# A gated delta rule and a gated MLP on one core: earlier masks for the triangular solve, filler matmuls, another dealing of VectorE's background work, and an early fetch for the last stage

## The chip, the core and the metric

The kernel runs on one core of one Trainium2 chip. The metric is the device time of one execution in microseconds (us). A core has five engines with their own instruction streams: TensorE (PE in the profile; its weight loads are listed as PEld), VectorE (DVE), ScalarE (ACT), GpSimd (POOL) and SyncE (SP). Transfers are issued from the queues of SP, POOL and ACT and run beside the engines.

## The reference

Two models follow one another; the output of the first is the input `x` of the second. Everything is float32.

```python
# B, H, S, D = 4, 8, 768, 48
k_n = k / (norm(k, axis=-1) + 1e-06)
state = zeros((B, H, D, D))
for t in range(S):
    y[:, :, t] = einsum('bhd,bhde->bhe', q[:, :, t], state)
    v_old = einsum('bhde,bhd->bhe', state, k_n[:, :, t])
    state = state + beta_t * einsum('bhd,bhe->bhde', k_n[:, :, t], v[:, :, t] - v_old)
x = y.transpose(0, 2, 1, 3).reshape(B, S, 384)
# d_model 384, d_ff 1024
h = gelu_tanh(x @ w_in)
u, v = h[..., :512], h[..., 512:]
v_n = (v - mean(v)) / sqrt(var(v) + 1e-06) * g_ln
v_s = einsum('ts,bsd->btd', w_sg, v_n) + b_sg[None, :, None]
out = x + (u * v_s) @ w_out
```

The first part is sequential in the 768 tokens, the spatial product `w_sg` mixes all tokens of a batch.

## The kernel before

**Chunks.** The recurrence is cut into 12 chunks of 64 tokens: six for the first two batches, six for the other two. Within a chunk the 64 steps become matrix products and the inverse of a triangular 64x64 matrix. Two chunks make a segment; the six segments have their own triangular inverses.

**Prologue.** `kload` and `qload` bring the keys and queries of a chunk (896 KB, issued on GpSimd's queue). `kgram`, `gram` and `dense` form the products of keys on TensorE, ScalarE copies them out of PSUM, `gstore` stores them to DRAM (`gd`), and `zload` brings them back with one 32x32 triangle per partition and block (`zl`). `lanes(g)` is VectorE's solve on that layout: read the diagonal, mask the upper triangle (`triu`, an affine_select on GpSimd, L317), a Newton inverse square root for the key norms, a scale, some 100 to 200 small steps over rows, outer products and columns, and a last scale. It comes in five groups: segments 0, 1, 2 with 3, 4, and 5. `zstore` stores the result (`zd`), `zfetch` brings it back as `z` and `zk`, `norms` turns the key norms into `nv`, `vprep` scales the values, `turned` transposes `zk`, and `corner_a` and `corner_b` put the off-diagonal 32x32 corners of the inverse together on TensorE.

**Turns.** The main part is a list of turns, each with a chunk c of the recurrence and a chunk f of the feed-forward part, either of which can be missing:

```python
TURNS: (0,None) (1,None) (2,None) (3,0) (None,1) (None,2) (4,3) (5,4) ... (11,10) (None,11)
```

In a turn with c the chain `old0, own0, state0, old1, own1, state1` runs, each step some 64 small matmuls that need what ScalarE or VectorE made of the step before; between the steps stand the eight `feeds` of chunk f (four `gate`, four `value`), that is matmuls with `w_in` and the gelu. In a turn without f nothing stands there. Towards the end of the turn the next chunk's `vprep`, `turned`, `corner_a` and `corner_b` follow.

**Background list.** VectorE's long work (the decoding of `w_in` into two float parts, the groups of `lanes`) waits in a list `bg`. After every step `tick` takes from it for as many estimated microseconds as the turn's entry in `SHARE` allots to the step, with an estimate per instruction of `us(n)`, 0.17 us plus n / 960. `until` takes all that is needed at once, where a turn can't go on without it (`lanes_done`). All engines work through their instructions in the order of the program, which is written by hand up to the last stage.

**Last stage.** `w_out` and `w_sg` are decoded or split by `unit`, six calls in a turn, in the last turns. After the turns come, for the four batches and two halves of tokens each, `fetch_v` (six pieces, normalised by ScalarE and VectorE), `fetch_u`, `spatial` and `project`. Here a scheduler sets the order. `keep_warm` issues matmuls of zeros whose result isn't read; before, it is called twice, 9 times at the start and 12 times ahead of turn 0 (with weights named `kick`).

## Time and profile before

| what | value |
|---|---|
| median of 3 runs | 601.35 us (600.41 to 605.57) |
| the profiled execution, its own time | 601.24 us |
| its span, first to last instruction | 599.3 us |
| mean granted TensorE clock | 0.826 of full |
| busy: TensorE, VectorE, ScalarE, GpSimd | 447.4, 360.8, 173.3, 74.7 us |
| matmuls | 7691 |
| first step of the chain of chunk 0 (L80, `ps<-v,z`) | at 86.5 us |
| last matmul of the feed-forward turns, first of the last stage | at 430.5 and 439.0 us |

The busy times are sums over stages with different limits; the profile says for each instruction group what ended the idle time before it, and in a table by stretches how busy each engine was there and which clock TensorE was granted (PEclk; 1.00 is full, 0.50 half).

### The profile page before, as it was taken

Reading aid. Unit: us, or ns where it says so; the run is one execution under the profiler, and the core shown is the slowest. Engines: PE = TensorE matmul, PEld = TensorE weight load, DVE = VectorE, ACT = ScalarE, POOL = GpSimd, SP = SyncE. Lnnn points to the kernel's source line nnn. Section 1 sums busy time; section 2 is a strip of 40 time slices with the busy share of each in tenths; the row PEclk is TensorE's granted clock in tenths of the full one; section 3 lists DMA queues with packets and bytes.
Section 4 is the critical chain, followed back from the end, with each engine's and each line's share of the span. In section 5 each row is a group of like instructions: output and inputs, shape, how many; then the busy total and the mean of one; then the engine's idle time right before and its main releaser. Section 6 shows DMA issues by size and latency. Waiting matters only on the chain.

```text
span 599.3 us, 17857 instructions
## 1 busy us (share of the span) xinstructions
PE 447.4 (75%) x7691; PEld 402.3 (67%) x7691; DVE 360.8 (60%) x1040; ACT 173.3 (29%) x382; POOL 74.7 (12%) x100
## 2 busy tenths in 40 slices
PE   4432088616948565899988991979769899999997
PEld 2432067615837454778877881868669899999997
DVE  3509583552799992766885763495645963643432
ACT  2310154112424212354424420443524421311110
POOL 3210021000030000201020100000002412222220
PEclk9655575555579875899999986997979999999999
DMA  7896285568347104886496726451787474423213
GB/s 235 179 279 159 57 211 149 115 177 170 108 125 229 70 18 133 219 233 212 118 226 193 194 84 180 121 189 47 259 231 184 125 236 132 152 56 129 83 58 118
DMA packets 99454, 92.79 MB, mean 155 GB/s; under 512 B 71600, under 2 KB 80432, under 8 KB 96912
## 3 DMA queue, kind: packets, MB, share of 16 engines
q1 hardware_dynamic: 89952, 58.40, 35.2%
q0 software_dynamic: 5312, 31.72, 19.0%
q10 hardware_dynamic: 4112, 1.54, 1.1%
q8 instruction: 60, 0.98, 0.7%
q14 instruction: 18, 0.15, 0.1%
HBM read 63.30 MB, written 28.34 MB: 153 GB/s over the span
## 4 chain that ended last, share of the span: by engine, by line
PE 52%; DVE 24%; DMA 12%; issue 6%; ACT 3%; SPq 2%; ACTq 0%; POOL 0%; DVEq 0%; POOLq 0%
PE ps L80 17%; PE ps L632 13%; PE ps L634 11%; PE ps L633 11%; DVE ztmp L357 4%; DVE zl L364 4%; DMA zd<-zl 3%; DMA kd<-kqT 3%; DMA vraw<-vD 3%; DMA gd<-gm 2%; DVE zl L351 1%; DMA z<-zd 1%; PE ps L654 1%; DVE zl L385 1%; DVE zl L341 1%
## 5 line engine op out<-in xcount | busy, mean ns | idle before, releaser
L80 PE MATMUL ps<-kd 48*64 48x128 f32 (+1 forms) x768 | 45.7, 357 | 46.8 <-DMA kd<-kqT 24.0
L80 PEld LDWEIGHTS ps<-kd 48*64 48x64 f32 x768 | 37.6, 189 | 49.6 <-ACT nv L402 21.5
L80 PEld LDWEIGHTS ps<-s,kq 48*64 48x64 f32 x1408 | 55.3, 159 | 17.6 <-issue 11.8
L80 PE MATMUL ps<-s,kq 48*64 48x48 f32 x1408 | 62.3, 245 | 4.0 <-issue 2.6
L1007 POOL TENSOR_TENSOR ga<-ga,uT 128x384 f32<-128x384 f32 x32 | 36.4, 1141 | 188.5 <-DVE ga L1004 139.9
L633 PE MATMUL ps<-xl,winh 128*128 128x256 f32 x144 | 43.4, 301 | 10.5 <-DVE xl L658 10.5
L357 DVE TENSOR_TENSOR ztmp<-zl 128x120 f32<-128x120 f32 (+26 forms) x180 | 48.4, 302 | 1.9
L364 DVE TENSOR_TENSOR zl<-zl,ztmp 128x120 f32<-128x120 f32 (+26 forms) x180 | 48.4, 301 | 0.9
L632 PE MATMUL ps<-xh,winh 128*128 128x256 f32 x144 | 46.6, 324 | 2.0 <-issue 2.0
L634 PE MATMUL ps<-xh,winl 128*128 128x256 f32 x144 | 42.8, 297 | 0.0
L80 PE MATMUL ps<-z,gm 32*32 32x32 f32 x768 | 11.6, 212 | 41.3 <-DMA z<-zd 39.0
L80 PE MATMUL ps<-v,z 64*64 64x48 f32 x768 | 33.7, 247 | 10.8 <-issue 5.2
L632 PE MATMUL ps<-wsgh,vnh 128*128 128x384 f32 x96 | 33.6, 350 | 9.3 <-ACT vnh L980 9.3
L499 DVE TENSOR_TENSOR v<-v,ps 128x384 f32<-128x384 f32 x22 | 12.0, 544 | 46.6 <-PE ps L80 46.6
L638 DVE TENSOR_TENSOR gl<-ga,gh 128x384 fp32r<-128x384 f32 x32 | 21.0, 656 | 31.3 <-ACT gh L637 31.3
L637 ACT CAST gh<-ga 128x384 fp32r<-128x384 f32 x32 | 16.4, 512 | 80.8 <-POOL ga L1007 80.6
L80 PEld LDWEIGHTS ps<-z,gm 32*32 32x32 f32 x768 | 9.8, 124 | 44.6 <-issue 43.4
L633 PEld LDWEIGHTS ps<-xl,winh 128*128 128x128 f32 x144 | 29.7, 206 | 11.5 <-DVE xl L658 11.1
L80 PEld LDWEIGHTS ps<-v,z 64*64 64x64 f32 x768 | 30.5, 161 | 10.3 <-DVE v L499 4.9
L80 PE MATMUL ps<-u,gm 64*64 64x48 f32 x768 | 34.8, 254 | 1.9 <-ACT u L521 1.9
L80 PE MATMUL ps<-u,kt 64*48 64x48 f32 x704 | 27.6, 243 | 9.5 <-ACT u L521 9.5
L80 PEld LDWEIGHTS ps<-u,gm 64*64 64x64 f32 x768 | 31.5, 169 | 3.8 <-ACT u L521 2.4
(126 smaller groups left out, 1163.3 us busy)
## 6 DMA issues: line engine op xcount, KB each, us to landing
kq<-kqT POOLq DMA_DIRECT2D x12, 896.0 KB, 9.3
kd<-kqT POOLq DMA_DIRECT2D x10, 896.0 KB, 9.2
vD<-vg SPq DMA_DIRECT2D x24, 256.0 KB, 3.2
uD<-ut SPq DMA_DIRECT2D x12, 512.0 KB, 4.4
vraw<-vD SPq DMA_DIRECT2D x48, 128.0 KB, 3.5
uT<-uD SPq DMA_DIRECT2D x8, 768.0 KB, 5.1
v<-vtok POOLq DMA_DIRECT2D x12, 384.0 KB, 6.1
kt<-ktok POOLq DMA_DIRECT2D x12, 384.0 KB, 8.3
```

Source lines behind the costliest of these rows:

```text
L80: return nc.tensor.matmul(out=out, lhsT=lhsT, rhs=rhs, start=start, stop=stop, skip_group_check=True)
L341: tv.tensor_tensor(out=z[:, a], in0=z[:, a], in1=nb[:, a].unsqueeze(2).broadcast_to([P, 32, 32]), op=ALU.mult)
L351: tv.scalar_tensor_tensor(out=z[:, a, 0:i, t], in0=z[:, a, 0:i, i], scalar=z[:, a, i, t:t + 1], in1=z[:, a, 0:i, t], op0=ALU.mult, op1=ALU ...
L357: tv.tensor_tensor(out=st["tmp"][:, at:at + m * (r1 - r0) * w].rearrange("p (m r t) -> p m r t", m=m, t=w), in0=z[:, :, r0:r1, i:i + 1].br ...
L364: tv.tensor_tensor(out=z[:, :, r0:r1, i + 1:32], in0=z[:, :, r0:r1, i + 1:32], in1=st["tmp"][:, at:at + m * (r1 - r0) * w].rearrange("p (m ...
L499: nc.vector.tensor_tensor(out=v[:, js[e]], in0=v[:, js[e]], in1=ks[e], op=ALU.add)
L632: nc.tensor.matmul(out=ps, lhsT=sh, rhs=mh, start=(first and i == 0), stop=False)
L633: nc.tensor.matmul(out=ps, lhsT=sh, rhs=ml, start=False, stop=False)
L634: nc.tensor.matmul(out=ps, lhsT=sl, rhs=mh, start=False, stop=(last and i == n - 1))
L637: nc.scalar.copy(out=hi, in_=src)
L638: nc.vector.tensor_tensor(out=lo, in0=src, in1=hi.bitcast(F32), op=ALU.subtract)
L1007: nc.gpsimd.tensor_tensor(out=gv, in0=gv, in1=uT[:, :, d], op=ALU.mult)
```

## The change

1. **The masks of groups 0 and 1.** For `lanes(0)` and `lanes(1)` the function `triu` is called when the group is created and no longer as its first step; its copy of the diagonal goes to ScalarE. `lanes(0)` is created right after its `zload`, and `kload(2)`, `kload(3)` and `qload(0)` are issued behind its mask on GpSimd's queue. `lanes(1)` is created after `dense(4)`, its mask is ahead of `kload(7)`, and its copy is ahead of the copies of `dense(5)` on ScalarE. The fetch of the first result stands behind ScalarE's copies for `norms` and `qgram`. Two loads of `w_in` move behind `qload(1)`. The first tick is for 11 us in place of 5.
2. **Filler matmuls.** In a turn without f each of the eight `feeds` places issues N_FILL = 3 matmuls of zeros, 128x128 by 512 columns in bf16. That is 24 places in turns 0 to 2, 72 matmuls.
3. **Dealing.** In a group of one segment an instruction is estimated at 0.13 us plus n / 960 where it was 0.17, and `SHARE` is larger in turns 0 to 2 and 6 to 9, so more is taken per turn.
4. **Turns 4 and 5.** Where a turn has no chunk c, what prepares the next chunk (fetch, norms, `vprep`, `turned`, both corners) moves behind the turn's feed-forward work.
5. **The last stage's weights** are begun one turn earlier, behind the end of `lanes(4)`.
6. **The last turn** (f = 11 alone) now fetches and normalises the six pieces of the first batch's v, one per `unit`, and loads the first uT. In the last stage uT has 2 buffers in place of 3, gh and gl 7 in place of 8.

```diff
         def triu():
-            tv.tensor_copy(out=d0, in_=dg)
+            (nc.scalar.copy if g < 2 else tv.tensor_copy)(out=d0, in_=dg)
...
+        if g < 2:
+            triu()
...
-            triu, *newton,
+            *([triu] if g >= 2 else []), *newton,
...
-        us = lambda n: 0.17 + n / 960
+        us = lambda n: (0.13 if m == 1 else 0.17) + n / 960
...
         gstore(c, (nc.sync, nc.scalar))
-        kload(c + 2)
...
     for _ in range(N_EARLY):
         win.pop(0)[0]()
+    first = lanes(0)
...
+    kload(2)
+    kload(3)
     qload(0)
     for c in (2, 3):
         dense(c)
...
     qload(1)
+    for k in (2, 3):
+        win_load(k, nc.gpsimd)
     dense(4)
     kload(6)
-    for op, _ in lanes(0):
+    bg += lanes(1)
+    dense(5)
+    kload(7)
+    for op, _ in first:
         op()
-    zfetch(0, nc.scalar)
     norms(0)
     for c in range(2):
         q0, q1 = qgram(c)
         deal([q0], [q1])
+    zfetch(0, nc.scalar)
+    dense(6)
     above(0)
     vprep(0)
-    bg += lanes(1)
-    dense(5)
-    kload(7)
-    dense(6)
-    tick(5.0)
+    tick(11.0)
...
-    SHARE = (9.0, 12.0, 11.0, 14.0, 16.0, 16.0, 11.0, 11.0, 11.0, 11.0, 11.0, 11.0)
+    SHARE = (12.0, 12.0, 12.0, 14.0, 16.0, 16.0, 14.0, 14.0, 14.0, 14.0, 11.0, 11.0)
...
                 spent({"value": f"part{i[-1]}"}.get(name, name))
+            else:
+                keep_warm(bank(), N_FILL, busy[:, 0:P])
...
+        if not ch and n is not None:
+            lanes_done(n // 2)
+            zfetch(n, nc.sync)
+            ready()
+            corner("corner_a")
+            corner("corner_b")
...
-        if c == NCH - 3:
+        if c == NCH - 4:
+            lanes_done(NSEG - 1)
+            norms(NSEG - 1)
             prep_ctx.close()
...
+        if at == len(TURNS) - 1:
+            main_ctx.close()
...
+            pieces, rests = fetch_v(0), []
+            for _ in range(3):
+                rests.append(pieces.pop(0)())
+            fetch_u(0, 0)
...
+            def v_unit():
+                rests.pop(0)()
+                if pieces:
+                    rests.append(pieces.pop(0)())
+                if units_w:
+                    units_w.pop(0)()
```

On GpSimd, at the start of the program, right behind the memsets of the two `z` buffers, this stood before (`kd` are the keys, `kq` keys and queries, `ut` raw `w_in`, `zl` the lane layout that L317 masks):

```order
L135 DMA kd_94<-kqT 112x2048
L135 DMA kd_95<-kqT 112x2048
L606 DMA ut<-w_in 128x1024 x2
L139 DMA kq_106<-kqT 112x2048
L135 DMA kd_94<-kqT 112x2048
L135 DMA kd_95<-kqT 112x2048
L147 DMA v_109<-vtok 128x768
L143 DMA kt_113<-ktok 128x768
L139 DMA kq_107<-kqT 112x2048
L135 DMA kd_94<-kqT 112x2048
L317 AFFINE_SELECT zl<-zl 128x1024
```

At the same place on GpSimd this stands now:

```order
L317 AFFINE_SELECT zl<-zl 128x1024
L135 DMA kd_94<-kqT 112x2048
L135 DMA kd_95<-kqT 112x2048
L139 DMA kq_106<-kqT 112x2048
L135 DMA kd_94<-kqT 112x2048
L135 DMA kd_95<-kqT 112x2048
L147 DMA v_109<-vtok 128x768
L143 DMA kt_113<-ktok 128x768
L139 DMA kq_107<-kqT 112x2048
L609 DMA ut<-w_in 128x1024 x2
L135 DMA kd_94<-kqT 112x2048
```

The first mask went from behind the load of the seventh chunk's keys to ahead of every load of this queue.

On TensorE, at the start of turn 0, the fillers (LDWEIGHTS and MATMUL of `busy`) now stand around the first step of the chain, `v,z`:

```order
L81 MATMUL ps<-j_798,ztk 32x32 x32
L81 MATMUL ps<-kd_95 64x128 x8
L98 LDWEIGHTS busy
L98 MATMUL ps<-busy 128x512
L98 LDWEIGHTS busy
L98 MATMUL ps<-busy 128x512
L98 LDWEIGHTS busy
L98 MATMUL ps<-busy 128x512
L81 MATMUL ps<-v_109,z_104 64x48 x16
```

Before, the rows of `v,z` came directly behind those of `kd_95`.

On VectorE this was the end of the last group of `lanes` (segment 5, chunks 10 and 11) before, followed in the next rows by the statistics of the first phase and then by the `vprep` (L472) and `turned` (L433) of chunk 10, the first chunk that needs it:

```order
L351 SCALAR_TENSOR_TENSOR zl<-zl 128x28 x3
L351 SCALAR_TENSOR_TENSOR zl<-zl 128x29 x2
L351 SCALAR_TENSOR_TENSOR zl<-zl 128x30
L389 MEMSET zl 128x32
L385 TENSOR_TENSOR zl<-zl,nb_3444 128x1024
L706 TENSOR_SCALAR ve<-mv 128x12
```

Now its end stands a few rows behind the `vprep` (L475) and `turned` (L436) of chunk 8:

```order
L475 TENSOR_TENSOR v_109<-v_109,nv 128x768
L436 STREAM_TRANSPOSE ztk<-zk 128x256
L354 SCALAR_TENSOR_TENSOR zl<-zl 128x26 x4
L354 SCALAR_TENSOR_TENSOR zl<-zl 128x27 x4
L354 SCALAR_TENSOR_TENSOR zl<-zl 128x28
L661 TENSOR_TENSOR xl<-ps,xh 128x3x128 x2
L354 SCALAR_TENSOR_TENSOR zl<-zl 128x28 x2
L354 SCALAR_TENSOR_TENSOR zl<-zl 128x29 x2
L354 SCALAR_TENSOR_TENSOR zl<-zl 128x30
L392 MEMSET zl 128x32
L388 TENSOR_TENSOR zl<-zl,nb_3584 128x1024
```

The group's end moved ahead by two chunks.

More of the change, by code (lines that the diff above doesn't have):

```diff
@@ L40 @@
 N_WARM = 9
+N_FILL = 3
 AHEAD = 7
@@ L715, in norm, with fetch_v, piece, rest @@
         return [(f, 0.2) for f in (first, *newton, last)]
+    late = None
+    g_sb = bsg_bc = None
+    TH = SEQ // 2
+    vns, uxs, gts = {}, {}, {}
+    def fetch_v(b):
+        nr = late.tile([P, NK, 2], F32, name="nrb", bufs=2)
+        for e in range(2):
+            nc.sync.dma_start(out=nr[TOK[e]], in_=nD[b // 2][TOK[1 - b % 2], :, e])
+        if b % 2 == 0:
+            vnh = late.tile([P, NT, DH], F32R, name="vnh")
+            vnl = late.tile([P, NT, DH], F32R, name="vnl")
+        else:
+            vnh, vnl = (w.rearrange("p a b -> p (a b)").rearrange("p (s d) -> p s d", d=DH)
+                        for w in (winh, winl))
+        vns[b] = vnh, vnl
+        def piece(st):
+            raw = late.tile([P, DH], F32, name="vraw", bufs=3)
+            for e in range(2):
+                nc.sync.dma_start(out=raw[TOK[e]], in_=vD[b // 2][st, e, TOK[1 - b % 2]])
+            def rest():
+                nc.scalar.activation(
+                    out=vnh[:, st], in_=raw, func=AF.Identity, scale=nr[:, st, 0:1], bias=nr[:, st, 1:2])
+                nc.vector.tensor_scalar(
+                    out=raw, in0=raw, scalar1=nr[:, st, 0:1], scalar2=nr[:, st, 1:2], op0=ALU.mult, op1=ALU.add)
+                nc.vector.tensor_tensor(out=vnl[:, st], in0=raw, in1=vnh[:, st].bitcast(F32), op=ALU.subtract)
+            return rest
+        return [lambda st=st: piece(st) for st in range(NT)]
@@ new lines, in fetch_u, with spatial @@
+    def fetch_u(b, th):
+        uT = late.tile([P, 3, ND, P], F32, name="uT", bufs=2)
+        nc.sync.dma_start(
+            out=uT.rearrange("p k d t -> p k (d t)"),
+            in_=uD[b // 2][3 * th:3 * th + 3, :, 1 - b % 2].rearrange("k p n -> p k n"))
+        uxs[b, th] = uT
+    def spatial(b, th):
+        vnh, vnl = vns[b]
+        uT = uxs.pop((b, th))
+        hs = slice(th * TH, th * TH + TH)
+        gt = []
+        for d in range(ND):
+            dsl = slice(d * P, d * P + P)
+            ps = bank()[:, 0:TH]
+            mm3(ps, [(vnh[:, st, dsl], vnl[:, st, dsl], wsgh[:, st, hs], wsgl[:, st, hs]) for st in range(NT)])
+            ga = late.tile([P, TH], F32, name="ga", bufs=3)
+            nc.vector.scalar_tensor_tensor(
+                out=ga, in0=ps, scalar=g_sb[:, d:d + 1], in1=bsg_bc[:, hs], op0=ALU.mult, op1=ALU.add)
+            gv = ga.rearrange("p (k t) -> p k t", t=P)
+            nc.gpsimd.tensor_tensor(out=gv, in0=gv, in1=uT[:, :, d], op=ALU.mult)
+            gh = late.tile([P, TH], F32R, name="gh", bufs=7)
+            gl = late.tile([P, TH], F32R, name="gl", bufs=7)
+            split(gh, gl, ga)
+            gt.append((gh, gl))
+        gts[b, th] = gt
@@ new lines, in project @@
+    def project(b, th):
+        gt = gts.pop((b, th))
+        for t3 in range(3):
+            tt = 3 * th + t3
+            x = late.tile([P, DM], F32, name="x", bufs=3)
+            for e in range(2):
+                nc.sync.dma_start(out=x[TOK[e]], in_=xD[b // 2][tt, TOK[1 - b % 2], e])
+            ts = slice(t3 * P, t3 * P + P)
+            ps = bank()[:, 0:DM]
+            mm3(ps, [(gt[d][0][:, ts], gt[d][1][:, ts], wouth[:, d], woutl[:, d]) for d in range(ND)])
+            o = late.tile([P, DM], F32, name="o", bufs=2)
+            nc.vector.tensor_tensor(out=o, in0=ps, in1=x, op=ALU.add)
+            nc.sync.dma_start(out=out[b, tt * P:tt * P + P, :], in_=o)
@@ L851, in delta_rule_gmlp_kernel @@
             tload(c + 1)
-        if n is not None and n not in zks:
+        if ch and n is not None and n not in zks:
             lanes_done(n // 2)
@@ L862, in delta_rule_gmlp_kernel, with ready @@
         does("gram")
-        if n is not None:
-            if n // 2 not in nvs:
-                until(lambda: n // 2 in ns)
-                norms(n // 2)
-            vprep(n)
-            turned(n)
-        corner("corner_a")
+        def ready():
+            if n is not None:
+                if n // 2 not in nvs:
+                    until(lambda: n // 2 in ns)
+                    norms(n // 2)
+                vprep(n)
+                turned(n)
+        if ch:
+            ready()
+            corner("corner_a")
         unit()
@@ L878, in delta_rule_gmlp_kernel @@
             gstore(c + AHEAD, (nc.sync,))
-        corner("corner_b")
+        if ch:
+            corner("corner_b")
         unit()
@@ L883, in delta_rule_gmlp_kernel @@
             ffn.moments(1)
+        if not ch and n is not None:
+            lanes_done(n // 2)
+            zfetch(n, nc.sync)
+            ready()
+            corner("corner_a")
+            corner("corner_b")
         if c == 1:
@@ L1034, in delta_rule_gmlp_kernel @@
             if b + 1 < NB and th == 0:
-                fetch_v(b + 1)
+                for piece in fetch_v(b + 1):
+                    piece()()
             spatial(b, th)
```

84 lines of the change are left out of this document (12 added, 72 removed).

## The prediction

> **What bounds the kernel now.** I read the page first: busy tenths and granted clock in 40 slices of 15 us, then what TensorE waited for.
>
> ```profile
> PE   4432088616948565899988991979769899999997
> PEclk9655575555579875899999986997979999999999
> PE ps L80 <- DMA z<-zd: 39.0, 3, 15.6
> PE ps L80 <- DMA kd<-kqT: 24.0, 3, 14.6
> PE ps L80 <- ACT nv L402: 21.1, 1, 21.1
> PE ps L632 <- ACT vnh L980: 9.3, 3, 8.1
> PE ps L634 <- DVE gl L638: 1.6, 1, 1.6
> ```
>
> The last ten slices (from 450 us) are TensorE at full clock, nearly without a stop. The first 15 (to 225 us) are another kernel: TensorE is half idle, the clock is mostly half, and it waits for loads and for what comes back from VectorE's solve (`z`, three long waits, 39.0 us). So I cut the span into stretches (columns: TensorE, weight loads, VectorE, ScalarE, GpSimd busy, then clock, DMA share, GB/s).
>
> ```profile
> 86.50:162.00 75.50, 48.57 (x1491) 43.77 (x1491) 37.48 (x134) 21.66 (x51) 4.92 (x9) 0.50 0.61 150
> 144.50:225.30 80.80, 54.07 (x997) 47.11 (x991) 70.88 (x141) 25.23 (x56) 6.89 (x10) 0.77 0.41 115
> 225.30:231.10 5.80, 0.01 (x1) 0.04 (x2) 1.40 (x3) 0.00 (x0) 0.00 (x0) 0.50 0.74 219
> 232.50:321.00 88.50, 80.27 (x2003) 67.96 (x2004) 59.00 (x217) 35.55 (x88) 10.05 (x16) 0.93 0.72 192
> 360.70:374.40 13.70, 1.29 (x65) 1.14 (x65) 4.58 (x17) 0.53 (x4) 0.00 (x0) 0.61 0.59 162
> 433.00:439.00 6.00, 0.04 (x1) 0.04 (x1) 2.65 (x15) 1.32 (x2) 0.00 (x0) 0.69 0.65 155
> 480.00:500.00 20.00, 20.00 (x116) 20.00 (x115) 11.68 (x22) 4.50 (x7) 4.39 (x4) 1.00 0.58 175
> ```
>
> Turns 0 to 3 run at half clock. At 225.3, 360.7 and 433 TensorE stands still, and once more ahead of 138 (its row is in term 2). From 144.5 to 225.3 VectorE is the bound (70.9 of 80.8 us); from 232 on TensorE is (80.3 of 88.5), and the last stage is at its pace of 116 matmuls in 20 us.
>
> **Term 1, up to turn 0.** These rows carry the first 87 us.
>
> ```profile
> 7.78 0.70 POOL L135 DMA_DIRECT2D kd<-kqT  x1 [2.91 <-PE ps L80]
> 21.84 0.34 SPq L298 DMA_DIRECT2D zl<-gd  x1
> 24.81 15.78 SPq L232 DMA_DIRECT2D gd<-gm  x8
> 27.49 0.19 DVE L315 COPY d<-zl 128x32 f32<-128x32 f32 x1 [2.06 <-DMA zl<-gd]
> 39.03 3.69 PE L80 MATMUL ps<-kd 48*64 48x128 f32 x64 [14.57 <-DMA kd<-kqT]
> 43.66 1.26 POOL L317 TENSOR_SCALAR_AFFINE_SELECT zl<-zl 128x1024 f32<-128x1024 f32 x1
> 44.96 1.22 DVE L341 TENSOR_TENSOR zl<-zl,nb 128x1024 f32<-128x1024 f32 x1 [13.75 <-POOL zl L317]
> 53.03 0.34 SPq L298 DMA_DIRECT2D zl<-gd  x1
> 67.42 1.23 DVE L385 TENSOR_TENSOR zl<-zl,nb 128x1024 f32<-128x1024 f32 x1
> 73.20 0.73 ACT L402 COPY nv<-ps 32x32 f32<-32x32 f32 x4 [29.38 <-issue]
> 77.07 0.18 DVE L315 COPY d<-zl 128x32 f32<-128x32 f32 x1
> kd<-kqT POOLq DMA_DIRECT2D x10, 896.0 KB, 9.2
> zl<-gd SPq DMA_DIRECT2D x6, 512.0 KB, 4.6
> gd<-gm SPq DMA_DIRECT2D x44, 64.0 KB, 5.4
> ```
>
> VectorE is ready for the mask at 44.96 - 13.75 = 31.2, but the mask stands in GpSimd's queue behind key loads that wait for products, and comes at 43.66: 13.75 us idle. With the mask first, the new order is as follows. No key loads run beside the first gram stores; at their median of 5.4 us the reload starts at about 17 to 18 in place of 21.84 and lands 4.6 later, at 22; the mask (1.26) hides beside Newton (3.7 us, 27.5 to 31.2), which ends at 27; scale and solve take 68.65 - 44.96 = 23.7, so group 0 ends at **51**, 18 us earlier.
>
> The price is paid by the loads behind the mask: `kd` for chunks 2 and 3 issues at 24 instead of 7.8 and lands at 33 to 35 (9.2 each). Two dense products of 3.7 us each put their stores on SP at 35 to 45, and the reload for group 1 follows when they land. I take 5.4 and 4.6 for store and reload, so group 1's lanes arrive at 52 to 55. The other end is before's own delay, 53.03 - 24.81 = 28 us from the first store to the reload, which gives 63 + 4.6 = 68; the median is nearer, since most of the loads that ran beside those stores now stand behind the keys of chunks 4 and 5, which wait for the same products. ScalarE waits for these lanes (its copy of the diagonal is ahead of `nv`), which takes the place of its 29.38 us behind the fetch. Then `nv`, `above`, `vprep`, and 11 us of dealt steps of group 1 on VectorE, until `turned(0)` at 67 to 69; two corners later the chain starts at 71 in place of 86.5: **-15.5** (with the late reload, about -3).
>
> **Term 2, turns 0 to 3.** The chain's steps wait for single copies, and the clock decides their length:
>
> ```profile
> 76.70:80.10 3.40, 3.40 (x61) 3.01 (x54) 3.11 (x10) 2.77 (x6) 2.32 (x3) 0.50 0.53 135
> 82.00:87.00 5.00, 3.42 (x164) 2.46 (x164) 4.93 (x18) 1.82 (x5) 0.00 (x0) 1.00 1.11 305
> 87.00:104.00 17.00, 14.40 (x474) 13.23 (x468) 6.31 (x30) 6.68 (x15) 2.19 (x4) 0.50 0.63 151
> L97 PE MATMUL ps<-busy x9: 607/634/635, 1.3 to 4.7; 128*128 128x512 bf16 x9
> L97 PE MATMUL ps<-busy,kick x12: 379/379/582, 79.9 to 82.5; 128*128 128x512 bf16 x12
> 86.52 0.31 PE L80 MATMUL ps<-v,z 64*64 64x48 f32 x3
> 88.53 0.32 PE L80 MATMUL ps<-u,kt 64*48 64x48 f32 x2 [0.57 <-ACT u L521]
> 105.22 0.44 PE L80 MATMUL ps<-v,z 64*64 64x48 f32 x3 [0.73 <-DVE zl L364]
> ```
>
> A stretch of 3.4 us filled to the brim (76.7 to 80.1) ends with full clock; one with 3.42 of 5.0 busy loses it; 14.4 of 17.0 at half clock does not win it back. Turn 0 takes 105.22 - 86.52 = 18.7 us. The 72 fillers cost, each, (4.7 - 1.3) / 8 = 0.43 us at half clock, and between 0.22 and 0.25 at full ((82.5 - 79.9) / 11 = 0.24, with some of both). Three per place fill the gaps of about 0.57 us that a copy leaves. So the bounds for all 72 are nothing (wholly in gaps, and the clock pays besides) and 72 x 0.43 = 31 us (half clock and nothing hidden). I expect that the clock, full after the kick, is held: of the 18.7 us, 18.7 x 14.4 / 17 = 15.8 are work, which halves to 7.9; the other 2.9 are waits; eight places with three fillers of 0.24 add 5.8, half of them in those waits; and I add 1 for value steps that queue on VectorE behind more dealt work: 7.9 + 2.9 + 2.9 + 1 = **14.7 us** per turn.
>
> The Trainium skill, "TensorE: Matmul & The Clock Gate", Part 1, has the gate released after one busy window of about 3.4 us, which the row at 76.7 bears out, and under "Why this matters for your kernels" it has the full clock lost by idle windows, "No PE-idle gaps >~3µs between matmul bursts". By that rule the clock would hold with or without fillers, the first rival below would have no chance, and turn 0 before would have run at full clock; the row from 82 to 87, with no such gap and the clock lost at its end, speaks against it here, and the sum goes by the row.
>
> The turns give group 1 its end:
>
> ```profile
> 126.67 1.23 DVE L385 TENSOR_TENSOR zl<-zl,nb 128x1024 f32<-128x1024 f32 x1
> 133.72 1.26 SPq L419 DMA_DIRECT2D zk<-zd  x2
> 138.07 1.29 PE L80 MATMUL ps<-z,gm 32*32 32x32 f32 x64 [15.61 <-DMA z<-zd]
> DVE v L499 <- PE ps L80: 26.5, 5, 5.9
> ```
>
> Before, VectorE began group 1 at 77.07 and ended it at 127.9, with 17 us of waits for TensorE's half-clock steps in between (the last row: 26.5 us in five) and what `until` forced at the end of turn 1 done beside an idle TensorE. Now a third is done ahead of turn 0, the rest is dealt into the two turns (SHARE 12 and 12, and a lower estimate per instruction, so more instructions), and the order has its end directly behind the last value step of turn 1. That is 71 + 14.7 + 7, about 93. From there as before: 5.8 us to the store's landing, 4.4 for the fetch, corner of chunk 2 at **103** in place of 138.1, 35 earlier, 19.5 beyond term 1. A longer turn from fillers would stay hidden as long as this round trip ends last: turn 1's own work ends at 71 + 29.4 = 100.
>
> From chunk 2's corner to the end of group 2 VectorE has the same 87.2 us (138.1 to 225.3), since decoding and group 2 may start only then. Turn 2's half clock is worth about 4 there, in its waits at the start. In turn 5 the transfers' 5.8 us of silence (225.3 to 231.1) now have feed-forward matmuls beside them, 2 of it net. So chunk 4 is reached at 190 in place of 231: **-25.5** for term 2 altogether, -41 with term 1.
>
> **Term 3, turns 6 to 14.** The stop at 360.7 comes from group 4 (segment 5), ended only where chunk 10 needs it, and 13.7 us long. In the new order its end is in turn 9, behind `turned` of chunk 8, two turns ahead of its use, so store and fetch are hidden. What it costs: some 16 us of VectorE's work moves from 321 to 361 into turns 6 to 9, where VectorE has 59.0 busy in 88.5. At (59 + 16) / 88.5 = 0.85 the chain's value steps queue behind dealt ones; bounds are nothing and all of the 13.7. TensorE remains the busier (80.3), so I take 2: **-12**.
>
> **Term 4, the seam.** TensorE's stop between 430.9 and 439.0 waits for the first piece of v. With three pieces fetched at the start of the last turn and all six normalised in it (ScalarE, VectorE beside matmuls), the seam closes: -8, and the half clock that follows the stop goes with it, about 1. The weights begun a turn earlier leave no `unit` over. Fewer buffers (uT 2, gh and gl 7) cost nothing if the second half-batch's last block isn't needed before the first projection has ended, one stage of about 19 us ahead; the nearest row is the last stage's pace, which they can lower at worst. I take 1 for both: **-8**.
>
> Sum: 601.24 - 41 - 12 - 8 = **540 us**, against the profiled execution, which is 0.1 below the median of the runs shown (its span is 1.9 less).
>
> **The rivals.** (a) *The fillers don't hold the clock*: three per place leave TensorE at 85 to 90% busy, which is what 87 to 104 had without winning full clock. Then turns 0 and 1 are 18.7 and some 6 of the 10 us of fillers each, group 1's wait no longer ends last, and chunk 2 starts at 71 + 50 = 121 in place of 103; VectorE's stretch hides turn 2's. 540 + 18 + 4 (the loss of turn 2's saving) = **562**. For it: 85% did not raise the clock. Against it: it is full at the start and only has to stay. (b) *The grams come late*: the stores again take what 53.03 - 24.81 shows, group 1 starts at 68, and TensorE's chain with it, 12.5 later: **552**. For it: the loads of chunks 2 to 4 and of the first queries follow one another closely now. (c) *VectorE becomes the bound in turns 6 to 9*, each value step late by some 2.5 us in four turns: 10 of the 12 are given back, **550**. (d) *Slower*: the seventh gh buffer. If the scheduler's order makes ScalarE wait at the fourth block of a half-batch for the projection of the one before, and the blocks behind it with it, TensorE loses up to a projection (36 matmuls of 20 / 116 = 0.172 us, 6.2) plus as much again at half clock after the stop, 12 in each of seven half-batches: 540 + 7 x 12 = **624**. It decides if the wait exceeds the stage of lead; before, TensorE's waits for gl are 1.6 us in all in that stage, so I hold it unlikely. (e) *Less is achieved than said*: group 1 is still unfinished at turn 1's end, or group 4 at chunk 10; each gives 8 to 12 back, 548 to 552, and goes with (b) and (c).
>
> **How the numbers follow.** Forecast 0.45 (526 to 550); (a) 0.18; (b) with its part of (e) 0.15; (c) with its part 0.11; (d) 0.03; two of the losses together, 565 to 595, 0.04; and 0.04 for better than 526 (grams earlier, or the clock full to turn 3). The range leaves out (d), the doubles and half of the better ones: **520 to 566**. A difference under 1%, 6 us, can hardly be told from none: faster by more than that 0.95, within it 0.02, slower 0.03 from (d).
>
> **What would show it.** The mask on GpSimd at about 22 and group 0's last scale at 50; the first chain step at 71 (late grams: over 80); PEclk near 1.0 in turns 0 and 1 with 14 to 15 us from one `v,z` of e = 0 to the next (24 or more: rival a); the end of group 1 before turn 1's; chunk 4's corner at 190; no TensorE stop over 5 us in turns 6 to 13, and under 21 us per turn there; the first spatial matmul within 1 us of the last gelu's, and 116 matmuls in 20 us after it. I am wrong if the stores and loads of the first 60 us collide, since every later term hangs on group 1's arrival.

## The result: 573.84 us against 601.34, a gain of less than half of what was forecast

| | before | after |
|---|---|---|
| median | 601.34 us (4 runs) | 573.84 us (568.98 to 575.35, 4 runs) |
| ratio, 95% interval | | 0.9525 [0.9458, 0.9592] |
| profiled execution, its span | 601.24, 599.3 us | 574.44, 572.7 us |
| mean granted clock | 0.826 | 0.875 |

Forecast were 540 us and a range of 520 to 566; the time lies above it. A run that took over 1.5% longer than the fastest of its kernel (one run each in two of the experiments and one of the kernel before) is left out of the ratios and kept in the medians and ranges. The page of the changed kernel, busy tenths of TensorE and the granted clock, in 40 slices of its own, slightly shorter span:

```profile
PE   4064529755847934989979879799999999999997
PEclk9555658786897978699989898899999999999999
```

The clock is higher in slices 7 to 11 (86 to 157 us), which are turns 0 to 2, but TensorE still stands often in the first 16 slices. Where the time went is seen at four marks of the two traces: the copy of the first corner of chunks 0, 4 and 11, and the last matmul of the feed-forward turns.

| stretch | before | after | difference | forecast |
|---|---|---|---|---|
| to chunk 0's corner | 83.6 | 83.9 | +0.3 | -15.5 |
| to chunk 4's corner | 148.9 | 147.5 | -1.5 | -25.5 |
| to chunk 11's corner | 161.8 | 154.7 | -7.1 | -12 |
| to the last feed-forward matmul | 36.2 | 29.3 | -6.9 | (none) |
| from there to the end | 168.8 | 157.4 | -11.4 | -8 |

The windows of the changed kernel that answer to those of before (TensorE, weight loads, VectorE, ScalarE, GpSimd busy, clock, DMA share, GB/s):

```profile
25.00:55.00 30.00, 17.00 (x321) 15.15 (x321) 23.23 (x116) 6.44 (x12) 4.29 (x8) 0.50 1.02 259
55.00:60.00 5.00, 0.00 (x0) 0.00 (x0) 0.00 (x0) 0.00 (x0) 0.00 (x0) 0.50 0.23 43
83.90:119.40 35.50, 30.77 (x838) 20.14 (x839) 18.65 (x78) 11.15 (x26) 2.19 (x4) 0.80 0.45 111
119.40:136.30 16.90, 4.86 (x168) 3.42 (x166) 1.44 (x3) 2.89 (x10) 1.62 (x3) 0.68 0.92 215
156.30:223.10 66.80, 44.27 (x640) 37.85 (x638) 60.37 (x120) 21.73 (x50) 5.69 (x8) 0.87 0.37 111
223.10:231.30 8.20, 1.35 (x64) 1.11 (x64) 3.78 (x9) 0.00 (x0) 0.00 (x0) 0.58 0.93 266
402.00:415.40 13.40, 13.40 (x112) 12.05 (x111) 4.97 (x10) 6.22 (x14) 0.00 (x0) 1.00 0.77 229
```

The reader is to see two things. From 25 to 55 us the transfer engines are full (share 1.02), and at the end all five engines wait for what they bring (55 to 60: nothing busy at all). And when group 1 has ended at 119.4, VectorE and TensorE mostly stand until chunk 2's corner copy, 16.9 us, where before it was 11.5 (127.9 to 139.4). At the other end, TensorE runs without a stop through the seam at 415.4.

The prologue's rows in the trace:

```profile
18.60 1.66 POOL L317 TENSOR_SCALAR_AFFINE_SELECT zl<-zl 128x1024 f32<-128x1024 f32 x1 [13.73 <-ACT d L315]
47.52 1.23 DVE L388 TENSOR_TENSOR zl<-zl,nb 128x1024 f32<-128x1024 f32 x1
32.40 16.00 SPq L232 DMA_DIRECT2D gd<-gm  x8
58.39 0.34 SPq L298 DMA_DIRECT2D zl<-gd  x1
58.78 8.35 SPq L232 DMA_DIRECT2D gd<-gm  x8
62.10 0.24 ACT L315 COPY d<-zl 128x32 f32<-128x32 f32 x1 [18.71 <-DMA zl<-gd]
67.23 2.86 SPq L413 DMA_DIRECT2D zd<-zl  x1
81.67 0.45 DVE L436 STREAM_TRANSPOSE ztk<-zk 128x256 f32<-128x256 f32 x1 [2.17 <-DMA zk<-zd]
```

The mask came even earlier than forecast (18.6) and group 0 ended at 48.75, 20 us earlier than before. The first step of the chain (`v,z`) came at 89.05, where 71 was forecast and 86.52 it was before. Group 0's result then lay for 18 us: the store is in SP's queue behind the reload of group 1, which waits until 58.39 for the gram stores, and behind eight more of these; it goes at 67.23. ScalarE waits until 62.10 for the same reload, and `nv` with it.

### The profile page after: what moved, and what is told of

Its sections match the earlier page's. It is cut to its first block, busy times and chain, and to the rows that moved or that the text cites. A ratio compares the mean times of both kernels' runs of the same rounds, so it can differ in the third digit from the quotient of the medians.

```text
span 572.7 us, 18004 instructions
## 1 busy us (share of the span) xinstructions
PE 452.6 (79%) x7763; PEld 393.9 (69%) x7763; DVE 361.2 (63%) x1038; ACT 173.0 (30%) x384; POOL 75.1 (13%) x100
## 4 chain that ended last, share of the span: by engine, by line
PE 57%; DVE 16%; DMA 15%; issue 6%; SPq 3%; ACT 3%; ACTq 1%; POOL 0%; DVEq 0%; POOLq 0%
PE ps L81 18%; PE ps L635 13%; PE ps L637 11%; PE ps L636 11%; DMA gd<-gm 4%; PE ps L98 3%; DMA kd<-kqT 3%; DMA zd<-zl 3%; DMA z<-zd 2%; DVE zl L367 2%; DVE ztmp L360 2%; DMA zl<-gd 1%; DMA vraw<-vD 1%; DMA bsg_bc<-b_sg 1%; ACT gm L287 1%
## 5 line engine op out<-in xcount | busy, mean ns | idle before, releaser
L81 PE MATMUL ps<-kd 48*64 48x128 f32 (+1 forms) x768 | 39.8, 332 | 29.2 <-DMA kd<-kqT 25.3
L81 PEld LDWEIGHTS ps<-s,kq 48*64 48x64 f32 x1408 | 50.2, 148 | 16.6 <-issue 10.6
L81 PE MATMUL ps<-s,kq 48*64 48x48 f32 x1408 | 56.6, 234 | 0.0
L81 PEld LDWEIGHTS ps<-kd 48*64 48x64 f32 x768 | 33.3, 175 | 33.5 <-DMA kd<-kqT 21.2
L287 ACT COPY gm<-ps 128x512 f32<-128x512 f32 x40 | 21.8, 590 | 49.4 <-PE ps L81 36.1
L81 PE MATMUL ps<-v,z 64*64 64x48 f32 x768 | 31.0, 235 | 7.1 <-DVE v L502 6.8
L81 PE MATMUL ps<-z,gm 32*32 32x32 f32 x768 | 10.9, 205 | 32.3 <-DMA z<-zd 20.3
L81 PEld LDWEIGHTS ps<-v,z 64*64 64x64 f32 x768 | 27.8, 149 | 8.6 <-DVE v L502 7.0
L81 PEld LDWEIGHTS ps<-z,gm 32*32 32x32 f32 x768 | 9.2, 116 | 35.2 <-issue 21.8
L635 PE MATMUL ps<-winh,xh 128*128 128x512 f32 x72 | 33.2, 461 | 0.0
L635 PE MATMUL ps<-wouth,gh 128*128 128x384 f32 x96 | 32.4, 340 | 0.2 <-ACT gh L640 0.2
L636 PE MATMUL ps<-wsgl,vnh 128*128 128x384 f32 x96 | 32.5, 339 | 0.0
```

What stands on the lines that cost most here:

```text
L81: return nc.tensor.matmul(out=out, lhsT=lhsT, rhs=rhs, start=start, stop=stop, skip_group_check=True)
L287: nc.scalar.copy(out=GM[c % N_M][:, js], in_=st["ps"])
L635: nc.tensor.matmul(out=ps, lhsT=sh, rhs=mh, start=(first and i == 0), stop=False)
L636: nc.tensor.matmul(out=ps, lhsT=sh, rhs=ml, start=False, stop=False)
```

## The experiments

Medians are of 4 runs each, ratios are to the kernel before on the same chip, with their 95% intervals; for comparison, the changed kernel's is 0.9525. Each profile is of one run, and the same code can differ from run to run: in three kernels below whose prologue is the changed kernel's (without fillers, with loads held, with the early fetch undone), chunk 0's corner came at 79.1 to 80.7 us, against 83.9 in the changed kernel's own profile.

**The queues of the prologue.** Two edits, apart and together. First, group 1's copy of the diagonal back on VectorE and its mask back in its list:

```diff
-            (nc.scalar.copy if g < 2 else tv.tensor_copy)(out=d0, in_=dg)
+            (nc.scalar.copy if g < 1 else tv.tensor_copy)(out=d0, in_=dg)
...
-        if g < 2:
+        if g < 1:
             triu()
...
-            *([triu] if g >= 2 else []), *newton,
+            *([triu] if g >= 1 else []), *newton,
```

> The changed kernel with group 1's mask and diagonal copy back in its own list (VectorE copies the diagonal), so ScalarE no longer waits for group 1's lanes (62.1 us) ahead of nv. Theory S, that chunk 0 is held by two things of which each alone suffices, ScalarE's wait for group 1's lanes and the store of group 0 in SP's queue behind the reload of group 1 and eight gram stores: z still arrives at 78 to 81, so 571 to 575 us. Rival V, that ScalarE's wait alone holds it: vprep of chunk 0 at about 51 in place of 67.2 and the time 8 to 12 us less, 562 to 566.

Measured: 572.0 us, 0.9504 [0.941, 0.9598]. `vprep` came at 50.2 in place of 67.2, and the time stayed the same: VectorE stood until group 1's lanes (62.7), the store still went at 64.3, and the transposition came at 75.6. Second, the store and chunk 0's fetch on ScalarE's queue, ahead of that copy:

```diff
-            nc.sync.dma_start(out=zd.rearrange(
+            (nc.sync if g else nc.scalar).dma_start(out=zd.rearrange(
...
-                (nc.sync if r else q).dma_start(
+                (nc.sync if r and c else q).dma_start(
...
+    for op, _ in first:
+        op()
+    zfetch(0, nc.scalar)
     bg += lanes(1)
     dense(5)
     kload(7)
-    for op, _ in first:
-        op()
...
-    zfetch(0, nc.scalar)
```

> The changed kernel with group 0's store and chunk 0's fetch on ScalarE's queue, ahead of the copy that waits for group 1's lanes; SP's queue no longer delays them. z lands at about 60 in place of 81. Theory S: nv and vprep stay at 64 to 68 and the 11 us of dealt steps follow, turned at 80, so at most 3 us less: 570 to 574. Rival W, that SP's queue alone holds chunk 0: the chain starts 10 or more earlier, 560 to 565.

Measured: 576.66, 0.959 [0.9508, 0.9671]. For chunk 0 this is theory S: the fetch of its z was issued at 60.35, and the transposition came only at 79.65, behind `nv`, `vprep` and the dealt steps. Both together:

> Both edits of the two kernels before together. Theory S: nv at about 57, vprep at 61, group 1's lanes at 62 and 11 us of its steps, turned at 73 to 74, first chain step at 77 to 79 in place of 89; group 1 ends 10 earlier and the time falls by 7 to 11: 563 to 567 us. Rival U, that group 1's late reload (58.4) holds everything behind it: under 3 us, 571 to 575.

Measured: 580.07, 0.9663 [0.96, 0.9725], not faster than either, with the transposition at 85.51 where theory S had 73 to 74; so the theory of the two queues fell. ScalarE's queue and its compute rows in that kernel say why:

```profile
48.83 0.34 ACTq L413 DMA_DIRECT2D zd<-zl  x1
60.04 1.34 ACTq L422 DMA_DIRECT2D zk<-zd  x2
65.38 1.95 ACTq L427 DMA_DIRECT2D z<-zd  x4
67.37 2.05 ACT L287 COPY gm<-ps 128x512 f32<-128x512 f32 x4 [24.86 <-DMA z<-zd]
```

The store was issued at 48.83, at once; its 512 KB had landed only when the fetch went at 60.04, 11 us later (in the kernel before, 68.67 to 71.28, 2.6 us). So it was not a queue that held it. ScalarE, which works in the order of the program, stood behind it for 25 us.

**Bytes.** So the transfers themselves were tried, first by moving two pieces of `w_in` and chunk 0's `kt`, 1.4 MB, behind group 1's mask:

```diff
-    tload(0)
     qload(1)
-    for k in (2, 3):
-        win_load(k, nc.gpsimd)
 ...
     bg += lanes(1)
+    tload(0)
+    for k in (2, 3):
+        win_load(k, nc.gpsimd)
```

> The changed kernel with 1.4 MB of loads (two pieces of w_in, chunk 0's kt) taken out of the burst of the prologue and put behind group 1's mask. Theory D, that the transfer engines, at a share of 1.0 from 25 to 55 us, set when the gram stores land and so group 1's reload: at 250 to 280 GB/s the 1.4 MB are 5 us, the reload comes at 50 to 53 in place of 55 to 58, chunk 0's corner 4 to 5 earlier, and the time is 568 to 571. Rival O, that the reload waits for the products and for SP's 16 us of issuing: reload at 55 to 58 and 572 to 576.

Measured: 575.44, 0.9565 [0.9515, 0.9616]. The reload came at 52.7, earlier as theory D has it, but the moved loads then ran beside group 0's store: issued at 61.47, it had landed at 77.8, and the corner copy was at 83.3, no earlier. The bytes had only changed place. Then with bytes left out, 2.5 MB, and every instruction and wait in its place (of the keys of chunks 4, 5 and 6 only 8 of 112 rows are loaded, so this kernel computes something else; it serves to time the transfers):

```diff
     def kload(c):
-            nc.gpsimd.dma_start(out=KD[c % N_2], in_=kqT[c])
+            r = 8 if c in (4, 5, 6) else 112
+            nc.gpsimd.dma_start(out=KD[c % N_2][0:r], in_=kqT[c, 0:r])
```

> The changed kernel with the key loads of chunks 4, 5 and 6 cut to 8 of 112 partitions (what is left out: these chunks' products are made of keys of earlier chunks), 2.5 MB less ahead of group 1's reload, in the order and with the waits of before. Theory D, that transfers are the bound from 25 to 55 us: at 270 GB/s 9 us less, the reload at 46 to 50 in place of 55 to 58, nv at 54 to 57, chunk 0's corner at 72 to 76 in place of 80 to 84, as term 1 of the prediction had it; 563 to 568 us. Rival O, that SP's issuing and the products set the reload: under 3 us of change there, 571 to 576.

Measured: 566.7 (562.17 to 571.85), 0.9401 [0.9333, 0.9469]; the profiled run took 562.17. SP's and ScalarE's rows of it:

```profile
49.39 0.34 SPq L299 DMA_DIRECT2D zl<-gd  x1
58.23 1.63 SPq L414 DMA_DIRECT2D zd<-zl  x1
71.96 0.37 ACT L454 COPY j<-ps 128x256 f32<-128x256 f32 x1 [3.49 <-PE ps L81]
```

and the window in which its transfer engines come free (share 0.45; 0.99 in the changed kernel):

```profile
45.00:50.00 5.00, 0.00 (x0) 0.00 (x0) 3.97 (x18) 0.00 (x0) 0.00 (x0) 0.75 0.45 137
```

The reload is 9 us earlier, and the corner copy at 72.0 in place of 83.9; term 1 had put it at 68. Chunk 11's corner came at 374.1 in place of 386.0, so the 12 us went through that far; the median is 7 us lower, with runs from 562 to 572. Against the three kernels with the same prologue (corner at 79.1 to 80.7) the gain is 7 to 9 us. One thing besides the bytes differs in the two profiles: here TensorE had the full clock from 20 to 45 us, in the changed kernel half. It is not the cause, since the kernel with the loads held, further below, had the full clock there too, and its reload came at 57.53. So the bytes ahead of the reload are the cause of most of term 1's loss.

**What the mask ahead of the loads is worth**: the key loads of chunks 2 and 3 first again, the mask behind them.

```diff
         gstore(c, (nc.sync, nc.scalar))
+        kload(c + 2)
 ...
-    kload(2)
-    kload(3)
     qload(0)
```

> The changed kernel with the key loads of chunks 2 and 3 ahead of group 0's mask on GpSimd again (issued at about 8), the mask behind them still ahead of all others. Theory D, that the transfer engines are the bound from 25 to 55 us and what the mask delays by 12 us comes back at their end: group 0 ends 3 to 6 us later (51 to 53), but the reload of group 1 comes at 48 to 53 in place of 58.4 and chunk 0's corner 4 to 8 us earlier; 565 to 570. Rival M, that the mask's place is worth its price as the prediction had it: group 0's later end delays chunk 0, 574 to 580.

Measured: 569.49, 0.9464 [0.9412, 0.9517]. Group 0's last scale is at 54.40, 6.9 us later than in the changed kernel, and the reload of group 1 at 55.8, within what the kernels with the changed kernel's order show (54.8 to 58.4); the time is not longer. So the earlier end of group 0 itself was worth nothing here. Theory D's 48 to 53 was too early, too: with these two loads back at 8 us the reload comes no earlier, so it is not their place that makes it late.

**The fillers.**

```diff
-N_FILL = 3
+N_FILL = 0
```

> The changed kernel with no filler matmuls (N_FILL 0). Theory F, that fillers hold the full clock in turns 0 to 2 and that VectorE's group 1, dealt along the chain of turns 0 and 1, feels it: those turns fall back to about 18.5 us each from about 16, group 1 ends 4 to 6 us later, turn 2 is covered by VectorE; 577 to 581 us. Rival R, that the fillers take in the chain what the clock gives: PEclk falls to 0.5 in 84 to 120, the time stays at 572 to 576. The prediction's own step would make it about 590.

Measured: 562.55, 0.9394 [0.9335, 0.9453]: none of the three; without fillers the kernel is 8 to 11 us *faster*. The window from chunk 0's corner to group 1's end (the changed kernel's is above, 83.90 to 119.40), and the timeline's rows of the fetch of chunk 2's z and of the loads beside it:

```profile
79.00:113.30 34.30, 26.30 (x801) 23.77 (x798) 18.87 (x78) 11.03 (x25) 2.19 (x4) 0.50 0.49 116
```

```profile
117.31 1.85 SPq L427 DMA_DIRECT2D z<-zd  x3
118.35 0.54 POOL L135 DMA_DIRECT2D kd<-kqT  x1 [3.68 <-PE ps L399]
118.89 0.54 POOL L139 DMA_DIRECT2D kq<-kqT  x1
```

and the same in the changed kernel:

```profile
123.10 0.54 POOL L135 DMA_DIRECT2D kd<-kqT  x1 [3.06 <-PE ps L399]
123.64 0.53 POOL L139 DMA_DIRECT2D kq<-kqT  x1
124.73 8.96 SPq L427 DMA_DIRECT2D z<-zd  x4
```

The fillers do hold the clock (0.80 against 0.50), yet the stretch takes 35.5 us with them and 34.3 without, with VectorE busy for about 18.8 us in both. TensorE is busy for 30.8 us with them and 26.3 without. The same window of the changed kernel for the fillers alone (L98) and for the chain's matmuls alone (L81; columns: TensorE, weight loads, clock, DMA share, GB/s) shows why:

```profile
83.90:119.40 35.50, 12.25 (x38) 2.98 (x39) 0.80 0.45 111
83.90:119.40 35.50, 20.23 (x800) 17.16 (x800) 0.80 0.45 111
```

The chain's own matmuls take 20.2 us in place of 26.3, and the fillers add 10.5 beside them. What the clock gave, the fillers took. And with them the fetch of z falls 1.1 us behind 1.8 MB of key and query loads and takes 9 us to issue; without them it is a microsecond ahead. To test that alone, the loads were held until chunk 2's z is complete, fillers kept:

```diff
+        if c == 2:
+            hold = const.tile([P, 32], F32, name="hold")
+            nc.gpsimd.tensor_tensor(out=hold, in0=Z[0][:, 0, 32:64], in1=Z[0][:, 1, 32:64], op=ALU.mult)
         if c is not None:
             vload(c + 1)
```

> The changed kernel with a small GpSimd product of two columns of chunk 2's z ahead of the loads for turn 3, so that these 2.2 MB start behind the fetch of z and not just ahead of it. Theory K, that with fillers group 1 ends so that the fetch (124.7) falls behind the key and query loads (123.1, 123.6) and crawls, 8.96 us on SP's queue in place of 1.3 without fillers: the fetch takes 2 to 4 us, chunk 2's corner copy comes at 127 to 129 in place of 136.3, VectorE's long stretch with it, 564 to 568 us. Rival L, that the fetch is slow because of the store's own landing or the gram stores: the corner stays at 134 to 137, and 572 to 576.

Measured: 566.84, 0.9456 [0.94, 0.9512], in theory K's range, though the interval overlaps the changed kernel's.

```profile
122.99 2.17 SPq L427 DMA_DIRECT2D z<-zd  x4
```

The fetch takes 2.2 us, and chunk 2's corner copy follows group 1's end by 9.2 us in place of 16.9 (8.4 without fillers). But from there to chunk 4 it takes 99.9 us in place of 95.0, with the loads for turn 3 late, so that chunk 4 stands only 1.0 us nearer to chunk 0 than in the changed kernel. Most of the 7 us by which this kernel's profiled run is shorter is therefore not the hold's: 3.2 lie ahead of chunk 0's corner, which the edit doesn't touch. Without fillers the distance from chunk 0's corner to chunk 4's is 140.6 against 147.5. So the meeting of fetch and loads is shown as what holds chunk 2 for 8 us; that it makes up the fillers' whole loss is not, since taking it away by a hold costs nearly as much elsewhere.

**The dealing** of before (0.17, smaller shares):

> The changed kernel with the estimates and the SHARE of before (0.17; 9, 12, 11 and 11 in turns 6 to 9). Theory of term 3: group 4 is again unfinished where chunk 10 needs it and TensorE stands there 8 to 13 us, against 2 to 4 us that turns 6 to 9 win back; 580 to 585 us. Rival N, that the larger shares cost in turns 6 to 9 what the stop cost: 572 to 577.

Measured: 581.96, 0.9691 [0.9654, 0.9727], 8 us slower. The stop in front of chunk 10 is back, in another form: VectorE works off the end of group 4 at once, and the first value step behind it waits, here from 345.9 to 353.3. The timeline's row that ends the stop, and the window in it (TensorE 0.00, VectorE 5.86 of 6.0 busy):

```profile
353.26 0.35 PE L81 MATMUL ps<-v,z 64*64 64x48 f32 x2 [7.37 <-issue]
```

```profile
346.00:352.00 6.00, 0.00 (x0) 0.00 (x0) 5.86 (x32) 0.11 (x1) 0.00 (x0) 0.60 0.00 0
```

Of these 7.4, turns 6 to 9 give back 4.8, so that from chunk 4's corner to chunk 11's it is 157.3 us against 154.7. That difference is within what kernels with the new dealing show for this stretch (153.0 with the loads held, 158.3 with the early fetch undone). The larger part of the loss lies earlier, in term 2's stretch: group 1 ends 41.1 us behind chunk 0's corner in place of 35.5, and chunk 4's corner comes 153.6 us behind it in place of 147.5.

**The last turn's fetch** undone (fetched behind the turns, the pools as changed):

```diff
-            pieces, rests = fetch_v(0), []
-            for _ in range(3):
-                rests.append(pieces.pop(0)())
-            fetch_u(0, 0)
...
-            units = [v_unit] * NT
...
     by_hand.close()
+    for piece in fetch_v(0):
+        piece()()
+    fetch_u(0, 0)
```

> The changed kernel with the first batch's v fetched after the turns, as before, and nothing taken into the last turn; all else as changed. Theory of the prediction's term 4: 8 us of seam and 1 of half clock return, 581 to 584 us. Rival: ScalarE and VectorE had room only because the work was spread over the last turn, and undoing it gives back 11 or more, over 585.

Measured: 580.06, 0.9658 [0.9623, 0.9692], 6 us slower, but not by the seam: the first spatial matmul is at 414.98, with no gap. The loss stands later:

```profile
435.00:455.00 20.00, 16.88 (x78) 15.73 (x76) 19.27 (x31) 9.13 (x15) 10.03 (x8) 0.83 0.54 140
```

Three waits for gh and gl, 0.9, 1.5 and 0.7 us, and half clock behind them; the changed kernel has 112 matmuls there. So the early fetch is worth these 6 us, but it is not what closed the seam. This kernel, like the changed one, keeps the feed-forward tiles (`fw`) open and lays the late tiles over the finished chain's alone; before, they lay over both. That this is what closed it was not tried by itself.

**A version that beats both.** (The expectations call these kernels x1 to x4, and "the kernel before" in them is the one just above.) VectorE's long stretch (group 1's end to group 2's, 103.7 us in the changed kernel, 97.4 before) holds 21.6 us of decoding `w_in` that could be done in VectorE's idle time. First, without fillers, two pieces decoded behind group 0 (x1):

```diff
-N_FILL = 3
+N_FILL = 0
...
+    for op, _ in first:
+        op()
+    for _ in range(6):
+        win.pop(0)[0]()
     bg += lanes(1)
     dense(5)
     kload(7)
-    for op, _ in first:
-        op()
```

> The changed kernel without fillers, and with two more pieces of w_in (10.8 us of VectorE) decoded right after group 0, in VectorE's idle time of 48 to 64 us, in place of after turn 1. Theory Q, that from the end of group 1 to the end of group 2 VectorE is the bound (98 us in the kernel without fillers), so that only work taken out of that stretch shortens it: 98 becomes 87 to 89, and 550 to 554 us against 562.6. Rival: the stretch follows TensorE's turns 2 to 5 and keeps 94 or more; 558 to 563.

Measured: 565.48, 0.9376 [0.9307, 0.9445], beyond the rival's time, and by the ratio the same as without fillers alone (0.9394). The stretch was 93.1 us in place of 98.1, but chunk 2's corner copy came 13.6 us behind group 1's end in place of 8.4: the fetch was issued at 123.7, a microsecond ahead of three loads, and its last piece landed beside them at 132.1. Chunk 0's corner, too, was later (83.7 against 79.1). Then two more pieces while that z is on its way (x2):

```diff
             zfetch(n, nc.sync)
+            if c == 1:
+                bg.extend(win)
+                tick(10.0)
...
-            bg.extend(win)
             bg.extend(lanes(2))
```

> The kernel before with the last two pieces decoded too while chunk 2's z is on its way back, 10.8 us of VectorE in a gap of about 8.4. Theory Q: another 6 to 9 us less in the stretch, the corner of chunk 2 up to 3 us later; 542 to 548 us. Rival: the decode delays chunk 2's vprep as much as it saves; 549 to 553.

Measured: 558.19, 0.9259 [0.9195, 0.9322], short of theory Q: group 2 ended 75.8 us behind group 1, but the corner of chunk 4 came 18 us later still, where it was 8 in the changed kernel. The third adds the order of the key loads (x3):

> The kernel before with the key loads of chunks 2 and 3 ahead of group 0's mask. With the decode in VectorE's idle time behind group 0, group 0's end (54 in place of 47) now counts, while the loads end earlier; theory D gives 1 to 4 us less than x2, the rival, that two pieces no longer fit ahead of vprep, up to 4 more.

Measured: **557.32 us, 0.9273 [0.9226, 0.9321]**, with x2 the fastest; the two can't be told apart. Its windows from chunk 2's corner to group 2's end and from there to chunk 4's corner:

```profile
127.30:193.40 66.10, 48.15 (x1087) 42.63 (x1087) 50.72 (x103) 22.90 (x49) 6.30 (x9) 0.73 0.54 145
193.40:213.10 19.70, 13.38 (x124) 11.76 (x124) 6.90 (x13) 4.17 (x12) 0.00 (x0) 0.76 0.66 187
```

In the second window it is no longer VectorE that holds chunk 4. TensorE works on feed-forward matmuls until 206.5 and then waits 5.3 us for a fetch of chunk 4's z that is issued at 207.4. That fetch is the second one: the same z was fetched from 195.2 on, as soon as group 2's store had landed, and the lines of change 4, which stand behind the feed-forward work of turns 4 and 5, fetch it again (50 pieces of z on SP's queue in place of 46). Leaving the second out was not tried.

The last four asked whether group 1's end follows the chain or the dealing. The transposition ahead of 8 us of dealt steps (x4):

> The kernel x3 (no fillers, w_in decoded behind group 0 and behind group 1, key loads first) with chunk 0's transposition ahead of the dealt steps, and 8 us of them in place of 11. In x3 the fetch of z lands at about 73 and the transposition waits on VectorE behind dealt steps until 81.6. Theory: the chain starts 6 to 8 earlier, group 1's end 2 to 6 earlier, 551 to 556 us. Rival: group 1, dealt later, ends no earlier, and the time stays at 556 to 559.

Measured: 564.83, 0.9358 [0.9293, 0.9424]: chunk 0's corner no earlier (84.0), group 1's end 7 us later (124.7): the rival, and slower than it said. With larger shares (17, 17):

> The kernel before with SHARE 17 in place of 12 in turns 0 and 1. VectorE has 18.7 busy of 34 us there in the kernel without fillers, so there is room. Theory, that group 1's end follows the dealing: it ends 3 to 6 earlier than in x4, 547 to 553 us. Rival, that the value steps of the chain queue behind dealt steps: within 2 of x4.

Measured: 560.08, 0.9331 [0.9281, 0.9382], within the intervals of x4. Group 1 did end 8 us earlier (116.7), so its end follows the dealing; but chunk 2's corner came 16.0 us behind it in place of 11.5. With the fillers on x4:

> The kernel x4 with the three fillers per place. Theory F, that fillers hold the clock and the loss is the fetch falling behind the loads alone: PEclk about 0.8 in turns 0 and 1 and, if the fetch of chunk 2's z is quick, 3 to 6 us less than x4; rival R, that they cost in the chain what the clock gives and delay the fetch too: 4 to 10 more than x4.

Measured: 562.99, 0.9381 [0.9338, 0.9424], neither. The fetch is quick there (3.6 us), the clock 0.80, and the time that of x4 within the intervals: where the fetch is not pushed behind loads, fillers neither win nor lose. Last, x3 with the larger shares, and with the two lines for `c == 1` moved out of the branch that x3 has them in:

> The kernel x3 with SHARE 17 in place of 12 in turns 0 and 1, the dealt steps ahead of chunk 0's transposition as in x3. Theory, that group 1's end follows how much of it is dealt and how early: it ends at 110 to 114 in place of 117.5, and 551 to 556 us against 557.3. Rival, that the chain's value steps queue behind it and chunk 2 starts no earlier: 556 to 560.

Measured: 559.53, 0.9292 [0.9228, 0.9357], the rival's time. Group 1 ended at 109.7 in place of 117.5, as the theory has it, but its store, issued at 110.8, had landed only when the fetch began at 118.1, 7.3 us later (2.6 in x3). The fetch of chunk 2's z was issued at 120.3 in place of 121.5, and its corner copy came at 129.5 in place of 127.3. The earlier end was lost in the store's landing; 2.2 MB of loads for the next turn had been issued from 103.8 to 105.4.

## Why the prediction was wrong, step by step

- **Term 1 (-15.5, measured +0.3).** The step that failed is "I take 5.4 and 4.6 for store and reload". These are medians over a kernel in most of which the transfer engines have room; from 10 to 50 us before they had none (share 0.97). The long landing, 28 us, stood in the prediction as "the other end" and was put aside because loads stood behind others in a queue. But the loads issued ahead of that reload are those of before in another order, and from 25 to 55 us the engines were full (share 1.02): the reload came at 58.4, and group 1's lanes at 62.1 in place of 52 to 55. The runs show the cause with the bytes taken away: the corner at 72.0. The prediction also has no term for group 0's own store, which waits in SP's queue until 67.23; the fetch behind it is issued 11 us later. Rival (b) had the mechanism, late grams, but not its size: it put group 1's lanes at 68, and the first chain step at 83.5 where 89.05 was measured.
- **Term 2 (-25.5, measured -1.5).** Two steps failed. The first is the turn, "15.8 are work, which halves to 7.9". The clock was not near 1.0, as forecast, but 0.79 in turn 0, where it was 0.50 without fillers. From corner to corner turn 0 took 17.7 us with fillers and 17.8 without: the chain's own matmuls took 11.7 us in place of 15.0, not half, and the fillers put 5.0 beside them, of which 1.8 fell into waits. So some 3 us were won and some 3 paid. Why the chain's matmuls shrink so little is open. In the prediction's own measure, from one `v,z` to the next, turn 0 took 21.4 us in place of 14.7; 3.75 of it is a stop that is shown in the last section. Group 1's end is 35.6 us behind chunk 0's corner in place of 44.3 before; 5.6 of that go with the new dealing (41.1 with the old shares), and none with the clock (34.3 at half of it). The second step is "From there as before: 5.8 us to the store's landing, 4.4 for the fetch", 10.2 to the first corner matmul; it was 15.6, because the fetch met the loads for turn 3. "A longer turn from fillers would stay hidden" left that meeting out. Behind it, VectorE's stretch from chunk 2's corner to group 2's end is 86.8 us, as assumed (87.2), but the 4 us that the clock of turn 2 was to take off it (it was 0.85) were not won, and turn 5's silence, 2 us less by forecast, stayed (8.2 us).
- **Rival (a)**: the clock was neither at half, as this rival has it, nor near full. Its time of 562 was nearer than the forecast's, but for another reason.
- **The rows on the clock.** The prediction reads the row from 76.7 to 80.1 as 3.4 us of work that end with full clock. TensorE was busy without a stop from 73.98 on, so the trace shows full clock after 6 us of work and not that 3.4 suffice. That the clock was lost at 87 without a long stop ahead of it is as the prediction says.
- **Term 3 (-12, measured -7.1)** had the stop right: TensorE's wait for chunk 10 is gone, and a stop of 7.4 us returns with the old dealing. The price of the larger shares in turns 6 to 9 was put at 2 us and came to about 5, half of what rival (c) has. Net, the dealing makes up only 2.6 of the 7.1 us, which is no more than runs differ here; what the other 4.5 come from was not tried.
- **Term 4 (-8)**: the seam closed (8.5 us to 0.2), and the last stage was 3.2 shorter; but the seam stays closed without the early fetch, so the step that named the fetch as what closes it failed, although the sum was near. What was not foreseen are 6.9 us in turns 13 and 14, where TensorE had waited in before (13.3 busy of 17.7 us from 394.3 to 412) and had the clock at 0.81; after, 15.7 of 16.0 at 1.00. The weights begun a turn earlier are a likely cause; that was not tried by itself.
- **Rival (d)** did not occur: the last stage keeps 115 matmuls in 20 us with seven gh buffers.
- **Luck**: terms 1 and 2 lost 39.8 us against the forecast and term 3 lost 4.9. That the sum missed by only 34 is owed to the 6.9 us in turns 13 and 14 and to 3.4 more than forecast at the end.

## What to carry to other kernels

A landing time is a property of the stretch as much as of the transfer: read the DMA share where the transfer will run, and where it is near 1.0 work with bytes over the GB/s of that stretch. Moving loads only helps if the engines have room where the loads go. And a faster step should be followed to the next transfers that it releases: here a fetch that stood a microsecond behind 1.8 MB took four times as long to issue as one that stood ahead. A gain in clock that is bought with work on the same engine has to be counted net: here some 3 us against some 3.
